# Routed attention and a gated feed-forward layer: picks over three steps, their mask factor on Pool, sums by halves, a deeper lead of scores in the first batch

## Chip, cores, metric

The kernel runs on one core of a Trainium2 chip. The metric is the time of one execution on the device in microseconds; below, the median of the runs shown is compared. The core's engines are TensorE (PE; its weight loads are listed as PEld), VectorE (DVE), ScalarE (ACT), GpSimd (POOL) and SyncE (SP, which here only issues DMAs). Each engine works through its own list of instructions in the order in which the program wrote them, and waits on semaphores for what other engines and DMAs deliver.

## What is computed

Two layers, one after the other, for 4 batches, 8 heads, 768 positions and 64 values per head:

```python
q_assign = argmax(normalised q . normalised centroids)      # 16 clusters per head
k_assign = argmax(normalised k . normalised centroids)
mask = q_assign[:, :, :, None] == k_assign[:, :, None, :]
scores = where(mask, scale * q @ k.T, -1e9)
attn = softmax(scores)                                      # + 1e-9 in the denominator
x = (attn @ v) laid out as (4 * 768, 512)
out = (sigmoid(x @ w_gate) * (x @ w_val)) @ w_out           # d_ff = 1536
```

The inputs are float32, and so is the output of 3072 x 512. The norm of q or k doesn't change which cluster wins, so only the centroids are normalised.

## The kernel before

**Steps.** The whole attention is a list of 384 steps written out by hand. A step is one block of scores: 128 keys of one head against 384 queries (`do_scores`, L467), an exp of it on ACT into an `es` tile (L472), and, some steps later, three small matmuls that add `es` times v to the head's accumulator (`do_av`, L484). A head has 12 steps, a pair of heads 24, a batch 96. `run_steps` writes for each step, in this order: the step's scores; a share of the feed-forward work that is waiting (`ffn_run`); the av of the step that lies `ahead` steps back; and then whatever was put on that step with `at(step, f)`. `ahead` is 3 in batch 0 and 2 later. The first two heads of batch 0 are interleaved (`first_steps`).

**The mask inside the scores.** Rows 64 to 79 of the transposed tile `T` of a head hold, for keys, a one-hot of the winning cluster, and for queries -1920 where the cluster is not the winning one. So the score matmul over 80 rows (128 in batch 0) adds -1920 wherever the clusters differ, and exp makes it zero. After a head's last av, `normalise` adds a tiny multiple of the sums of v (`SV`), takes the reciprocal of the sum column and scales: L235 and L236 on DVE, L237 on POOL (on DVE for the last head of batch 0). The tile `xp` of two heads is then transposed into `xT`, by DMA (L499) or, for the last pair of batch 0, by PE (`by_pe`, L507, L508).

**Preparing a pair, batches 1 to 3** (`pair_prep`, for the pair whose scores begin at step `use`, from step `s0` on, with `gap` steps between its two heads): the loads of k, q and v by SP (L111); `sp`, a split of k (side 0) or q (side 1) into a half-precision high part (L743, on DVE for the first three pairs and on POOL after that) and the remainder (L744, POOL); `turn`, a DMA transpose into `T` (L257); `lgt`, the matmuls with the centroids into one PSUM bank (L273) and a copy of their low part by ACT (L279); `pk`, the pick, all on DVE in one step: the sum of the two parts (L304), the maximum (L285), two compares into a one-hot tile (L291), and the factor -1920 on the query side (L298); `ot`, the transpose of the one-hot tile (L761 by DMA, L323 and L759 by PE for the first pair); and `hops`, four small DMAs that put the one-hots into rows 64 to 79 of the two `T` tiles (L327). `v_cast` (POOL, L187 and L188) makes the v operand, `v_sum` the sums of v: one reduction on DVE (L194) and later a matmul (L200) and a scaling (L205). `first` holds the starting steps of the first three pairs (load, `s0`, `gap`); for the others they are use-76, use-58 and 10.

**Preparing a pair, batch 0.** PE does the transposes (`turn_pe`, L595, with the copy out at L596), the picks (`a_pick`) take two heads at once and have no mask factor (it comes with the copy out, in `place` or as `slot_f` in `a_place`, L639), `a_place` transposes the one-hots on PE (L323) and hops them, and the sums of v come from PE (`v_sum_pe`, L212). The first two heads are prepared ahead of step 0 by the code at L671 to L702, with dummy matmuls (`dummies`, L558) between the parts; `split` there makes high and low parts (L572, L574), and `first_place` copies the first one-hots (L629 on DVE, L627 on ACT).

**Feed-forward.** The work of a batch is cut into atoms (`ffn_atoms`): gate matmuls (L341) and a tanh (L347, ACT), value matmuls (L356) and the product `hT` (L361, DVE), and output matmuls (L373) with copies out (L380, L382). `ffn_run` deals them out over the steps of the next batch; what is left runs after the last step. In batch 0 there are none to deal out.

**Buffers.** PSUM has a `ring` of four banks for scores, gate, value, logits and, from step 96 on, everything that `prep_bank` gives out; two banks for av; two (`op`) for outputs and, before step 96, the preparing work. `es` tiles come from a pool of 6.

The pool's depth, the lead and the order in a step are set by these lines:

```python
esp = pool("es", 6)
...
while len(pend) > ahead:
    do_av(pend.pop(0))
run_bg(step_no[0])
...
first = {96: (45, 54, 6), 120: (50, 68, 8), 144: (62, 84, 10)}
ld, s0, gap = first.get(use, (use - 76, use - 58, 10))
...
run_steps([(24, first_steps)] + heads(0)[2:], x0, 0, None, ahead=3)
```

Of the kernel before, what the change touches and what calls it, by code (L numbers as in the profile page):

```python
# [8 lines left out]
FP = mybir.dt.float32  # L9
# [7 lines left out]
def kernel(  # L17
# [11 lines left out]
    nc = tc.nc  # L29
# [27 lines left out]
    ohp = pool("oh", 2)  # L57
    esp = pool("es", 6)
    tmpp = pool("tmp", 2)
# [130 lines left out]
    def v_sum(b, p):  # L190
        s = svp.tile([128, 2, 65], HP, tag="vs", name="vs")
        POOL.memset(s[:, :, 64:65], float(NCH))
        with nc.allow_low_precision("sums of the fp16 values' sources"):
            DVE.tensor_reduce(  # L194
                s[:, :, 0:64], RAW["v", b, p].rearrange("p h c d -> p h d c"), AX.X, ALU.add
            )

        def rest():
            t = bank(130, name="vs_ps")
            PE.matmul(  # L200
                out=t, lhsT=ones, rhs=s.rearrange("p h d -> p (h d)"), start=True, stop=True
            )
# [4 lines left out]
        return rest  # L207

# [78 lines left out]

    def mark(lg, mx, parts, mask=True):

        for a, z, nh, key, o in parts:  # L290
            DVE.tensor_tensor(  # L291
                o,
                lg[:, a:z].rearrange("p (h c) n -> p h c n", h=nh),
                bcast(mx[:, a:z].rearrange("p (h c) -> p h c", h=nh), NCL),
                ALU.is_equal if key else ALU.is_lt,
            )
            if mask and not key:
                DVE.tensor_scalar(o, o, MASK, None, ALU.mult)  # L298

    def pick(lg, parts, mask=True):  # L300
        if isinstance(lg, tuple):
            ls = smp.tile([128, 12, NCL], FP, name="lgs")
            n = lg[0].shape[1]
            DVE.tensor_tensor(ls[:, 0:n], lg[0], lg[1], ALU.add)  # L304
            lg = ls[:, 0:n]
        mark(lg, top(lg), parts, mask)

# [167 lines left out]
    def do_av(s):  # L475
# [34 lines left out]
        if last_x:  # L510
            at(step_no[0] + 4, by_pe)
        elif b == 0:
            at(47 + 4 * p, by_dma)
        else:
            by_dma()
# [3 lines left out]
    def at(i, f):  # L519
        bg.setdefault(max(i, step_no[0]), []).append(f)  # L520
# [97 lines left out]
    def a_pick(p):  # L618
        oh = st0["oh", p] = new_oh()
        pick(st0["lg", p], [(0, 12, 2, True, oh_view(oh, 0, 2, 2, 6)),  # L620
                            (12, 24, 2, False, oh_view(oh, 1, 2, 2, 6))], mask=False)

# [25 lines left out]
    def first_pick(e):  # L648
        lg, oh = st0["lg0", e], ohs[0]
        mark(lg, top(lg), [(0, 6, 1, True, oh_view(oh, 2 * e, 1, 1, 6)),  # L650
                           (6, 9, 1, False, oh_view(oh, 2 * e + 1, 1, 1, 3))], mask=False)

# [10 lines left out]
    def rest_pick():  # L663
        pick(st0["lgr"], [(0, 6, 2, False, oh_view(ohs[1], 0, 2, 1, 3))], mask=False)

# [18 lines left out]
    centroid_d(cv)  # L684
    split(1, 0, 6, POOL, POOL)
    split(1, 6, 9, POOL, POOL)
    dummies(2)
    turn_pe([(0, 0, 6)], ACT)
    turn_pe([(0, 6, 3)], DVE)
    dummies(2)  # L690
    first_logits(0)
    v_cast(0, 0, ACT)
    for e in range(2):
# [25 lines left out]
    for p in range(1, NP):  # L719
# [9 lines left out]
        at(l_at[3], lambda p=p: a_pick(p))  # L729
        at(l_at[3] + 2, lambda p=p: a_place(p, (0,) if p == 1 else ()))  # L730
        at(U - 9, lambda p=p: v_cast(0, p))
        at(U - 5, lambda p=p: v_sum_pe(0, p))
# [3 lines left out]
    def pair_prep(b, p, use, s0, gap):  # L736
# [11 lines left out]

        def pk(e):
            if e == 0:  # L750
                st["oh"] = new_oh()
            pick(st["lg", e], [(0, 6, 1, True, oh_view(st["oh"], 2 * e, 1, 1, 6)),
                               (6, 12, 1, False, oh_view(st["oh"], 2 * e + 1, 1, 1, 6))])

# [11 lines left out]

        lead = 10 if gap < 10 else 12
        for e in range(2):
            s = s0 + gap * e
            at(s, lambda e=e: sp(e, 0))  # L770
            at(s + gap // 2 - 1, lambda e=e: sp(e, 1))
            at(s + gap - 1, lambda e=e: turn((b, 2 * p + e), st["hl", e], tp))
            at(s + gap + lead, lambda e=e: lgt(e))
            at(s + gap + lead + 1, lambda e=e: pk(e))
        s = s0 + 2 * gap + lead + 2
        at(s, ot)
# [3 lines left out]
        at(use - 20, lambda: v_cast(b, p))  # L780
        at(use - 15, lambda: st.update(f=v_sum(b, p)))
        at(use - 6, lambda: st["f"]())

    for b in range(1, B):
        for p in range(NP):
            use = 96 * b + 24 * p
            first = {96: (45, 54, 6), 120: (50, 68, 8), 144: (62, 84, 10)}
            ld, s0, gap = first.get(use, (use - 76, use - 58, 10))
# [50 lines left out]
```

## Time and profile before

| | |
|---|---|
| median of 8 runs | 354.46 us (354.14 to 356.18) |
| the profiled execution | 354.14 us, its span 352.4 us |
| mean granted TensorE clock | 0.985 of full speed |
| TensorE busy | 328.2 us (93% of the span) |
| ScalarE busy | 232.7 us (66%) |
| VectorE busy | 172.8 us (49%) |
| GpSimd busy | 123.3 us (35%) |
| exp of one step (L472) | 497 ns, 384 of them |
| scores of one step (L467) | 333 ns listed, 384 of them |
| split remainder (L744, POOL) | 914 ns, 48 of them |
| sums of v (L194, DVE) | 1484 ns, 12 of them |
| mask factor (L298, DVE) | 423 ns in the mean, 24 of them |
| compares of the picks (L291, DVE, 96 elements) | 325 ns in the mean, 48 of them |

How to read it: the page of the profile lists for each engine the busy time, its share of the span and the number of instructions; a table by stage does the same for stretches of the span, with the TensorE clock that was granted (1.00 is full speed) and the share of time in which the DMA engines were busy. A row of waits says which engine and line waited for which, then us in total, how often, and the longest. A row of the timeline has the start in us, the length in us, engine, line, operation, output<-input, shapes, the count, and in brackets the idle time of the engine before it and what ended that. A "q" after an engine's name is its instruction queue, so "SPq" rows are DMA issues. Matmuls overlap in the array, so the listed duration of one is longer than its share of the engine's time.

### The profile page before, as it was taken

Reading aid. Unit: us, or ns where it says so; the run is one execution under the profiler, and the core shown is the slowest. Engines: PE = TensorE matmul, PEld = TensorE weight load, DVE = VectorE, ACT = ScalarE, POOL = GpSimd, SP = SyncE. Lnnn points to the kernel's source line nnn. Section 1 sums busy time; section 2 is a strip of 40 time slices with the busy share of each in tenths; the row PEclk is TensorE's granted clock in tenths of the full one; section 3 lists DMA queues with packets and bytes.
Section 4 is the critical chain, followed back from the end, with each engine's and each line's share of the span. In section 5 each row is a group of like instructions: output and inputs, shape, how many; then the busy total and the mean of one; then the engine's idle time right before and its main releaser. Section 6 shows DMA issues by size and latency. Waiting matters only on the chain.

```text
span 352.4 us, 8568 instructions
## 1 busy us (share of the span) xinstructions
PE 328.2 (93%) x3276; PEld 203.1 (58%) x3276; DVE 172.8 (49%) x395; ACT 232.7 (66%) x533; POOL 123.3 (35%) x199
## 2 busy tenths in 40 slices
PE   7797875889999999999999999999999999999995
PEld 3476643656655665565656566556655665565552
DVE  5486643765564547346554566455634232342230
ACT  5676875787867787677867787578876884332321
POOL 4896464335353445314353535333211000000000
PEclk9999997799999999999999999999999999999999
DMA  7999999495473398666765299433413010300102
GB/s 215 331 201 211 270 216 237 96 218 175 102 220 80 95 220 223 106 124 182 102 180 128 92 225 198 116 87 69 78 25 96 30 24 10 103 1 32 60 0 89
DMA packets 81000, 46.44 MB, mean 132 GB/s; under 512 B 60832, under 2 KB 77888, under 8 KB 80960
## 3 DMA queue, kind: packets, MB, share of 16 engines
q1 hardware_dynamic: 76960, 40.99, 47.7%
q0 software_dynamic: 3712, 4.72, 7.9%
q8 instruction: 25, 0.41, 0.5%
q10 hardware_dynamic: 288, 0.20, 0.2%
q14 instruction: 15, 0.12, 0.1%
HBM read 28.34 MB, written 6.29 MB: 98 GB/s over the span
## 4 chain that ended last, share of the span: by engine, by line
PE 73%; DVE 5%; DMA 3%; issue 2%; ACT 1%; POOL 1%; DVEq 0%; POOLq 0%
PE o L373 17%; PE v L356 17%; PE g L341 17%; PE sc L467 12%; PE av L484 7%; DMA T<-hl 3%; DVE hT L361 2%; PE lg L273 2%; DVE oh L291 1%; DMA T<-ohT 1%; DVE mx L285 1%; DVE t L235 0%; DVE lgs L304 0%; ACT th L347 0%; DVE vs L194 0%
## 5 line engine op out<-in xcount | busy, mean ns | idle before, releaser
L472 ACT ACTIVATE es<-sc 128x384 f16<-128x384 f32 x384 | 173.8, 497 | 53.0 <-PE sc L467 37.1
L467 PE MATMUL sc<-T 80*128 80x384 f16 (+1 forms) x384 | 119.8, 333 | 3.2 <-DVE hT L361 1.8
L484 PEld LDWEIGHTS <-es 128*128 128x128 f16 x1152 | 82.5, 99 | 47.4 <-ACT es L472 3.6
L361 DVE SCALAR_TENSOR_TENSOR hT<-th,v 128x384 f16<-128x384 f32 x96 | 52.8, 553 | 98.9 <-PE av L484 57.9
L484 PE MATMUL av<-va,es 128*128 128x65 f16 x1152 | 99.2, 196 | 0.0
L356 PE MATMUL v<-xTb,wv 128*128 128x384 f16 x384 | 78.1, 325 | 1.7 <-DVE hT L361 1.3
L237 POOL TENSOR_TENSOR xp<-t,rec 128x384 f16<-128x384 f32 x31 | 25.7, 830 | 150.2 <-DVE rec L236 145.1
L341 PE MATMUL g<-xTb,wg 128*128 128x384 f16 x384 | 78.0, 325 | 0.3
L373 PE MATMUL o<-wo,hT 128*128 128x512 f16 x288 | 70.6, 378 | 0.0
L347 ACT ACTIVATE th<-g 128x384 f32<-128x384 f32 x96 | 47.4, 494 | 26.6 <-DVE hT L361 16.2
L341 PEld LDWEIGHTS <-wg 128*128 128x128 f16 x384 | 37.3, 97 | 24.5 <-issue 3.2
L356 PEld LDWEIGHTS <-wv 128*128 128x128 f16 x384 | 37.3, 97 | 23.7 <-issue 3.5
L373 PEld LDWEIGHTS <-hT 128*128 128x128 f16 x288 | 27.9, 97 | 25.5
L467 PEld LDWEIGHTS <-T 80*128 80x128 f16 (+1 forms) x384 | 37.5, 98 | 0.6 <-DVE T L629 0.5
L744 POOL TENSOR_TENSOR hl<-qraw,hl 128x384 f16<-128x384 f32 x24 | 21.9, 914 | 13.1 <-DVE hl L743 11.6
L382 ACT ACTIVATE ob<-o 128x512 f32<-128x512 f32 x16 | 9.6, 598 | 22.3 <-PE o L373 22.3
L744 POOL TENSOR_TENSOR hl<-kraw,hl 128x384 f16<-128x384 f32 x24 | 21.9, 913 | 4.6 <-PE av L484 1.7
L235 DVE TENSOR_TENSOR t<-av,sv 128x390 f32<-128x390 f32 x32 | 18.0, 562 | 11.2 <-PE av L484 9.8
L194 DVE TENSOR_REDUCE vs<-vraw 128x128 f16<-128x768 f32 x12 | 17.8, 1484 | 0.0
L380 DVE TENSOR_SCALAR ob<-o 128x512 f32<-128x512 f32 x8 | 5.5, 692 | 22.2 <-PE o L373 22.2
L273 PE MATMUL lg<-cm,T 128*128 128x32 f16 x288 | 11.0, 177 | 4.1 <-DMA T<-hl 4.1
L304 DVE TENSOR_TENSOR lgs<-lg,lglo 128x192 f32<-128x192 f32 x24 | 8.2, 343 | 12.6 <-ACT lglo L279 12.3
(84 smaller groups left out, 216.0 us busy)
## 6 DMA issues: line engine op xcount, KB each, us to landing
vraw<-in_v_dram SPq DMA_DIRECT2D x16, 384.0 KB, 5.4
out_dram<-ob SPq DMA_DIRECT2D x24, 256.0 KB, 2.2
kraw<-in_k_dram SPq DMA_DIRECT2D x15, 384.0 KB, 3.8
qraw<-in_q_dram SPq DMA_DIRECT2D x15, 384.0 KB, 4.3
wg<-in_moe_w_gate_dram POOLq DMA_DIRECT2D x2, 768.0 KB, 10.3
wv<-in_moe_w_val_dram POOLq DMA_DIRECT2D x2, 768.0 KB, 13.3
wo<-in_moe_w_out_dram POOLq DMA_DIRECT2D x4, 384.0 KB, 15.6
T<-ohT SPq DMA_DIRECT2D x58, 24.0 KB, 1.9
```

Source lines behind the costliest of these rows:

```text
L235: DVE.tensor_tensor(t, av, sv, ALU.add)
L237: eng.tensor_tensor(x, t[..., 0:64], bcast(r, 64), ALU.mult)
L273: PE.matmul(out=lg[:, bass.ts(c, 32)], lhsT=t[:, c, :], rhs=cm[:, h].rearrange("p s n -> p (s n)"), start=True, stop=True,)
L341: PE.matmul(out=g[:, 0:n], lhsT=wg[fc // WQ][:, dc, fc % WQ, :], rhs=xT[:, dc, t0 : t0 + n], start=(dc == 0), stop=(dc == NDC - 1),)
L347: ACT.activation(th[:, 0:n], g[:, 0:n], AF.Tanh, scale=0.5)
L356: PE.matmul(out=w[:, 0:n], lhsT=wv[fc // WQ][:, dc, fc % WQ, :], rhs=xT[:, dc, t0 : t0 + n], start=(dc == 0), stop=(dc == NDC - 1),)
L361: DVE.scalar_tensor_tensor(hT[:, fc, 0:n], st[0][:, 0:n], 1.0, w[:, 0:n], ALU.add, ALU.mult)
L373: PE.matmul(out=o, lhsT=hT[:, fc, bass.ts(t, 128)], rhs=wo[fc // 3][:, fc % 3, :], start=(fc == 0), stop=(fc == NFC - 1),)
L467: PE.matmul(out=sc.rearrange("p (c t) -> p c t", t=128), lhsT=s["k"], rhs=s["q"], start=True, stop=True,)
L472: ACT.activation(es, sc, AF.Exp, scale=SCALE)
L484: PE.matmul(out=av[:, s["c0"] + i, :], lhsT=s["es"][:, bass.ts(i, 128)], rhs=VA[b, p][:, e, s["j"], :], start=(first and i == 0), stop=(la ...
L744: POOL.tensor_tensor(hl[:, :, 64:128], r, hl[:, :, 0:64], ALU.subtract)
```

## The change

1. **Picks of batches 1 to 3 in three steps.** `pk` no longer runs in one step: in the first, the sum and the maximum (L304, L285); in the second, the compare of the key side; in the third, the compare of the query side, and its factor -1920, which moves from VectorE to GpSimd. `mark` and `pick` lose their mask argument. `ot` follows two steps later, and so do the hops. `lead`, the steps from a head's transpose to its logits, becomes 12 for all pairs (it was 10 where `gap` is under 10), and the `gap` of the first pair of batch 1 becomes 5.
2. **Sums of v by halves.** `v_sum` reduces one head at use-17 and the other at use-14, in place of both at use-15. GpSimd's small memset moves to use-17 with it.
3. **First batch.** `ahead` is 4 (3 before), the pool of `es` tiles has 7. `a_place` comes 5 steps after the pick (3 for the second pair; it was 2), `v_cast` 18 steps before the pair's end of preparation (it was 9), and the PE transposes of the last `xp` five steps after it (it was 4).
4. **Before step 0.** The high parts of the second head's first k and q parts are made by ACT (POOL before), two single dummies stand where two pairs stood, the copy of the first transposed k goes to DVE (ACT before), and the second head's q part is split after the first logits.

```diff
-    esp = pool("es", 6)
+    esp = pool("es", 7)
...
-        with nc.allow_low_precision("sums of the fp16 values' sources"):
-            DVE.tensor_reduce(
-                s[:, :, 0:64], RAW["v", b, p].rearrange("p h c d -> p h d c"), AX.X, ALU.add
-            )
+
+        def half(e):
+            with nc.allow_low_precision("sums of the fp16 values' sources"):
+                DVE.tensor_reduce(
+                    s[:, e, 0:64], RAW["v", b, p][:, e].rearrange("p c d -> p d c"), AX.X, ALU.add
+                )
...
-            if mask and not key:
-                DVE.tensor_scalar(o, o, MASK, None, ALU.mult)
...
-            at(step_no[0] + 4, by_pe)
+            at(step_no[0] + 5, by_pe)
...
-    split(1, 0, 6, POOL, POOL)
-    split(1, 6, 9, POOL, POOL)
-    dummies(2)
-    turn_pe([(0, 0, 6)], ACT)
+    split(1, 0, 6, ACT, POOL)
+    dummies(1)
+    turn_pe([(0, 0, 6)], DVE)
     turn_pe([(0, 6, 3)], DVE)
-    dummies(2)
+    dummies(1)
     first_logits(0)
+    split(1, 6, 9, ACT, POOL)
     v_cast(0, 0, ACT)
...
-        at(l_at[3] + 2, lambda p=p: a_place(p, (0,) if p == 1 else ()))
-        at(U - 9, lambda p=p: v_cast(0, p))
+        at(l_at[3] + (3 if p == 1 else 5), lambda p=p: a_place(p, (0,) if p == 1 else ()))
+        at(U - 18, lambda p=p: v_cast(0, p))
...
-        def pk(e):
-            if e == 0:
+        def pk(e, i):
+            if e == 0 and i == 0:
                 st["oh"] = new_oh()
-            pick(st["lg", e], [(0, 6, 1, True, oh_view(st["oh"], 2 * e, 1, 1, 6)),
-                               (6, 12, 1, False, oh_view(st["oh"], 2 * e + 1, 1, 1, 6))])
+            if i == 0:
+                st["ls", e] = total(st["lg", e])
+                st["mx", e] = top(st["ls", e])
+            elif i == 1:
+                mark(st["ls", e], st["mx", e],
+                     [(0, 6, 1, True, oh_view(st["oh"], 2 * e, 1, 1, 6))])
+            else:
+                o = oh_view(st["oh"], 2 * e + 1, 1, 1, 6)
+                mark(st["ls", e], st["mx", e], [(6, 12, 1, False, o)])
+                POOL.tensor_scalar(o, o, MASK, None, ALU.mult)
...
-        lead = 10 if gap < 10 else 12
+        lead = 12
...
-            at(s + gap + lead + 1, lambda e=e: pk(e))
-        s = s0 + 2 * gap + lead + 2
+            for i in range(3):
+                at(s + gap + lead + 1 + i, lambda e=e, i=i: pk(e, i))
+        s = s0 + 2 * gap + lead + 4
...
-        at(use - 15, lambda: st.update(f=v_sum(b, p)))
-        at(use - 6, lambda: st["f"]())
+        at(use - 17, lambda: st.update(f=v_sum(b, p)))
+        at(use - 17, lambda: st["f"][0](0))
+        at(use - 14, lambda: st["f"][0](1))
+        at(use - 6, lambda: st["f"][1]())
...
-            first = {96: (45, 54, 6), 120: (50, 68, 8), 144: (62, 84, 10)}
+            first = {96: (45, 54, 5), 120: (50, 68, 8), 144: (62, 84, 10)}
...
-    run_steps([(24, first_steps)] + heads(0)[2:], x0, 0, None, ahead=3)
+    run_steps([(24, first_steps)] + heads(0)[2:], x0, 0, None, ahead=4)
```

More of the change, by code (lines that the diff above doesn't have):

```diff
@@ L205, in rest @@
             DVE.tensor_scalar(sv.rearrange("p h d -> p (h d)"), t, TINY, None, ALU.mult)
-        return rest
+        return half, rest
     def v_sum_pe(b, p):
@@ L286, in top, with mark @@
         return mx
-    def mark(lg, mx, parts, mask=True):
+    def mark(lg, mx, parts):
         for a, z, nh, key, o in parts:
@@ L296, in mark, with total, pick @@
             )
-            if mask and not key:
[L298 to L306, printed above, removed]
+    def total(lg):
+        ls = smp.tile([128, 12, NCL], FP, name="lgs")
+        n = lg[0].shape[1]
+        DVE.tensor_tensor(ls[:, 0:n], lg[0], lg[1], ALU.add)
+        return ls[:, 0:n]
+    def pick(lg, parts):
+        mark(lg, top(lg), parts)
     oh_n = [0]
@@ L620, in a_pick @@
         pick(st0["lg", p], [(0, 12, 2, True, oh_view(oh, 0, 2, 2, 6)),
-                            (12, 24, 2, False, oh_view(oh, 1, 2, 2, 6))], mask=False)
+                            (12, 24, 2, False, oh_view(oh, 1, 2, 2, 6))])
     def place(t, ps, slot, c0, n, key, eng):
@@ L650, in first_pick @@
         mark(lg, top(lg), [(0, 6, 1, True, oh_view(oh, 2 * e, 1, 1, 6)),
-                           (6, 9, 1, False, oh_view(oh, 2 * e + 1, 1, 1, 3))], mask=False)
+                           (6, 9, 1, False, oh_view(oh, 2 * e + 1, 1, 1, 3))])
     def first_place(e):
@@ L663, in rest_pick @@
     def rest_pick():
-        pick(st0["lgr"], [(0, 6, 2, False, oh_view(ohs[1], 0, 2, 1, 3))], mask=False)
+        pick(st0["lgr"], [(0, 6, 2, False, oh_view(ohs[1], 0, 2, 1, 3))])
     def rest_place():
```

## The prediction

> **What bounds the kernel now.** I read the page's engine shares first, then a table by stage, then who waits for whom on TensorE, and last two stretches of the timeline. The page says that TensorE is the engine to watch:
>
> ```profile
> PE 328.2 (93%) x3276; PEld 203.1 (58%) x3276; DVE 172.8 (49%) x395; ACT 232.7 (66%) x533; POOL 123.3 (35%) x199
> PEclk9999997799999999999999999999999999999999
> ```
>
> By stage (stretch, then busy us and count of PE, PEld, DVE, ACT, POOL, granted clock, DMA share, GB/s), with cuts at the first score, before and after the worst hole, at the full feed-forward load and at the last attention step:
>
> ```profile
> 12.00:52.00 40.00, 33.55 (x576) 25.09 (x575) 25.89 (x59) 30.01 (x69) 28.48 (x40) 1.00 1.09 235
> 52.00:72.00 20.00, 14.40 (x181) 10.13 (x180) 10.82 (x31) 13.16 (x32) 9.12 (x13) 0.74 0.72 169
> 90.00:296.00 206.00, 202.04 (x1993) 125.02 (x1992) 102.89 (x225) 152.80 (x356) 71.89 (x118) 1.00 0.53 120
> ```
>
> Busy overstates TensorE, so I also went through the starts of its matmuls. Back to back they lie 0.162 us apart for 384 columns, 0.216 for 512, 0.030 for the 65-column av; time beyond that I call lost. Lost: 5.1 us in 0-12, 10.5 in 12-52, 10.4 in 52-72 (half clock included), 1.9 in 72-90, 8.4 in 90-296, 0.1 after: 36.4 of 352.4. This is all that a change of order can give back. In batch 0 (steps 0-95, to 72 us) there is no feed-forward work to fill holes; a plain step there runs at ScalarE's pace, (3.95-0.49)/9 = 0.384 us per exp (ten in 3.95 us), against 0.25 us of TensorE.
>
> Later batches: one pick in two puts a clump on VectorE.
>
> ```profile
> 100.05 0.84 DVE L291 TENSOR_TENSOR oh<-lgs,mx 128x96 f16<-128x96 f32 x2
> 100.86 0.91 POOL L744 TENSOR_TENSOR hl<-kraw,hl 128x384 f16<-128x384 f32 x1
> 100.92 0.89 DVE L298 TENSOR_SCALAR oh<-oh 128x96 f16<-128x96 f16 x1
> 101.73 1.01 DVE L361 SCALAR_TENSOR_TENSOR hT<-th,v 128x384 f16<-128x384 f32 x2
> 102.33 0.32 PE L467 MATMUL sc<-T 80*128 80x384 f16 x1 [0.61 <-DVE hT L361]
> ```
>
> The mask L298 needs 0.19 us alone and 0.89 beside Pool's L744; two hT are held behind it, their PSUM banks stay taken, and TensorE waits. I count such holes at 101, 138, 159, 178, 197, 215, 236 and 256 us: 6.3 of the 8.4 us lost there.
>
> Batch 0 ends with the other large hole. SyncE's queue and what waits for it:
>
> ```profile
> 48.09 2.43 SPq L327 DMA_DIRECT2D T<-ohT  x4
> 50.61 1.91 SPq L257 DMA_TRANSPOSE T<-hl  x1
> 52.57 0.57 SPq L111 DMA_DIRECT2D kraw<-in_k_dram  x1
> 53.20 0.50 SPq L111 DMA_DIRECT2D qraw<-in_q_dram  x1
> 53.75 0.46 SPq L111 DMA_DIRECT2D vraw<-in_v_dram  x1
> 54.33 2.64 SPq L257 DMA_TRANSPOSE T<-hl  x1
> ```
>
> ```profile
> PE lg L273 <- DMA T<-hl: 4.1, 3, 3.4
> PE vs_ps L212 <- POOL va L188: 2.5, 2, 1.6
> PE oh_ps L323 <- DVE oh L291: 2.4, 3, 0.8
> ```
>
> SyncE issues without a pause; the last transpose lands 6.25 us after its issue (the chain of waits), at 60.6, and the logits of step 76 stand on TensorE from 57.1 to 60.6. The other two rows (us, times, longest) are a_place and v_sum_pe, which come before their data.
>
> **What the Trainium skill says.** "SBUF — State Buffer", section Who interferes with whom: VectorE and GpSimd share one port pair under an exclusive lock; a two-port-mode op or one with two SBUF inputs blocks fully against a Pool instruction, a tensor_reduce never. The trace agrees: L298 is 188 ns at its fastest and 893 at its slowest, L291 245 and 552, L194 always 1471 to 1496. "Perfetto Trace Analysis", per-instruction lifecycle, DMA HWDGE: an issue's profiled window is not the transfer; here 2.64 us against 6.25. "TensorE: Matmul & The Clock Gate", What's actually happening: after an idle window the array runs at half rate; here the granted clock is 0.74 in 52-72.
>
> **The change, part by part.**
>
> Picks. There are 24. L298 leaves VectorE: 10.2 us in total. On Pool it is an operation the trace lacks (96 halves from SBUF, one input). Lower bound 0.17 us (the 128x12 memset L187), upper 0.55 (the 192-element two-input L574); from Pool's casts L572 (344 ns at 192, 527 at 384) I take 344-96x0.95 = 0.25, so 6 us on an engine 35% busy. It waits there for mark's second compare. Queued behind it are the next pair's L743/L744, three steps later; their transpose is due 5 steps after those, their logits 18, so nobody waits. At the first head of each pair VectorE now runs t 0.56, rec 0.19, lgs 0.32, mx 0.35, two oh 0.84, mask 0.89 = 3.2 us ahead of the next hT. After: 1.4 us in the first step, then a compare of 0.26 (up to about 1.1 if locked out by L744) in each of the next two, an hT able to go between. The one pick with no Pool work beside it (256 us, 2.0 us of clump) lost 0.31, and the second heads' picks of about 1.3 us lost nothing, so about 1.7 us are free. I keep 0.15 us per place, 8 x 0.15 = 1.2 of 6.3, and round the gain to **5.0**. The bounds are all of it, 6.3, and minus 3.5 (rival 3). The one-hot transpose and hops move two steps later; hops still issue 11 steps (9 us) before use and land in 2-4 us: 0.
>
> Sums. L194 becomes two. The fixed part from L285: 353 ns at 192 elements, 554 at 384 (another row of that line) gives 152; a half is (1484-152)/2+152 = 0.82 us. VectorE pays 12x0.15 = 1.8 us in all, hidden (49% busy). It was on the path once, at 78-81 us, where TensorE lost 0.29: gain **0.3**.
>
> Prologue. Two dummies go (0.43 us of PE); the k copy moves from ACT (0.78) to DVE (0.55); ACT takes casts of 0.51 and 0.35, Pool sheds 0.64 and 0.34. The first score (11.57) waits for ACT's place L627 at 11.04, which is queued behind casts that waited for q's DMA until 10.09. ACT's queue is as long as before (0.86 for 0.78) and still reaches those casts early. Gain **0**; from -0.3 to +0.4.
>
> Batch 0 to step 54. a_place(1) one step later, a_place(2) and (3) three; v_cast nine steps earlier. Holes at 25.1 (0.98), 27.3 (1.49), 33.7 (0.95) and 38.4 (1.06) would shrink to some 0.9 in all; those at 45.9 and 50.6 come after. But head 4's hops now leave later by step. The pick is done at 34.66, or about 33.0 once 1.7 us are saved before it; step 36's transposes, ohT (0.62) and two issues put the second hop at 35.2; hops there take 4.6 us to land (DMA share over 1): 39.8, when step 48's score was at 41.54. So the first 3.6 us are capped: **1.5** (0.5 to 3.5). A fourth score ahead covers 4x0.384 = 1.54 us of TensorE's absence for ScalarE instead of 1.15, which helps only up to the same landing.
>
> Step 54 to 76. Pool takes v_cast (0.97 us) before the splits, in a gap it had (2.57 us idle before 43.8). SyncE now issues the first transpose, then four hops, then three loads, then the second transpose: 1.9+2.4+1.6 us as before, starting when q's low part is ready, 3.4 us after step 54, where the hops started before (48.1). So the second transpose again issues near 9.6 and lands near 15.8 us after step 54's start. TensorE arrives at step 76 earlier (holes of 0.95, 1.79 and 0.51 gone, 3.2 us) and waits that much longer: **0**. Step 72 now waits for hops queued behind the transpose, inside the same wait.
>
> Step 76 to 104. The one-hot transposes lost 1.12 and will wait some 0.3; but the logits of the next pair's second head, two steps later, again meet their transpose (issued after the hops, landing about 10.6 us after step 76): **0.4**. The last xp of batch 0 no longer stands behind a pick on VectorE, and its transposes come one step later: 0.81 lost becomes 0.3: **0.5**.
>
> Sum: 5.0+0.3+0+1.5+0+0.4+0.5 = 7.7 us. The profiled execution took 354.14 us (span 352.4 and 1.7 around it), 0.3 below the median of 354.46; 354.14-7.7 = **346.4**.
>
> **Rivals.**
> 1. Batch 0 is not tied to SyncE. For: 20.9 us are lost in 12-72; against: six queue entries without a gap. If hops and transposes keep up, the 3.6 and 3.2 us both count, less the 1.5 already in: 346.4-5.3 = **341.1**.
> 2. The steady gain is only half: compares locked out by L744 at 0.9 us still delay hT. For: Pool's split begins one step after the first-head pick. 346.4+2.5, and nothing from batch 0 (+1.5): **350.4**; without any steady gain, 353.5, near no change.
> 3. Slower: the port lock at the second heads. Their compares move to the steps in which Pool starts the next pair's split, where formerly they were over. t, rec, then a compare of 0.26+0.9 is 1.9 us, with a mask on Pool after it. If the clump at both heads goes past about 2.5 us, each first head keeps its 0.8 and each second head gains one of 0.4: 8x0.4 = 3.2 more lost, batch 0 nothing: **357**. It decides when the compares, not the mask, are what Pool blocks.
>
> **Numbers.** Main case 0.57, rival 1 0.20, rival 2 0.13 (0.02 of it within 0.2%), rival 3 0.10. A measurement of this kernel can tell about 0.2%, 0.7 us. Faster 0.88, same 0.02, slower 0.10. Low end: rival 1's price, 341.1; high end: rival 2 with almost no gain left, 352.5. Left out: rival 3 and what is beyond rival 1.
>
> **What would show it.** Right: L298's line on Pool near 0.25 us, no TensorE wait for hT over 0.3 us in 90-290, lost time there near 3 us; SyncE again unbroken before the second T<-hl, a wait on it of 5 us or more at step 76, half clock once more after it. Wrong: logits of step 76 not waiting for the transpose (rival 1), L291 near 1 us and hT waits as before (rivals 2 and 3), or a first score not at 11.6.

## Result and the profile after

The changed kernel takes **349.51 us** in the median (11 runs, 348.97 to 351.79), the kernel before 354.54 us (32 runs). The ratio is 0.986 [0.9841, 0.988]: about 5.0 us faster, inside the range of the prediction, but 2.7 us less than its 7.7. In one of the experiments below (the loads behind the turn) the profiled execution was disturbed, so its time and its profile are not used.

The profiled execution has a span of 347.3 us (352.4 before), which is again 5.1 us. The page's engine shares and its line of granted clocks, after:

```profile
PE 325.4 (94%) x3274; PEld 203.7 (59%) x3274; DVE 160.2 (46%) x384; ACT 232.5 (67%) x534; POOL 134.7 (39%) x221
PEclk9999896799999999999999999999999999999999
```

VectorE has lost 12.6 us of work and Pool has taken 11.4. Neither number is the gain. The table by stage shows where time went (stretch, then busy us and count of PE, PEld, DVE, ACT, POOL, granted clock, DMA share, GB/s):

```profile
12.00:50.20 38.20, 32.84 (x562) 25.76 (x559) 23.57 (x58) 28.16 (x65) 26.20 (x37) 0.96 1.14 239
50.20:67.00 16.80, 9.98 (x123) 7.09 (x121) 7.68 (x21) 9.69 (x24) 8.41 (x13) 0.70 0.77 164
85.00:291.00 206.00, 205.49 (x2050) 128.01 (x2049) 95.50 (x224) 156.55 (x366) 84.59 (x141) 1.00 0.53 126
```

The last row answers to 90 to 296 us of before: of 206 us TensorE is now busy in 205.49, where it was 202.04, and runs 57 more matmuls in the same time. The first two rows are no better than before: the clock is 0.96 where it was 1.00, and 0.70 where it was 0.74.

The starts of single scores put numbers on this. Score n is the block of scores of step n, counted from 0; lengths are between starts, in us:

| from score to score | before | after | gained | forecast |
|---|---|---|---|---|
| start to 54 | 44.34 | 45.89 | -1.55 | +1.5 |
| 54 to 77 (the long wait of step 76 in it) | 16.62 | 16.31 | +0.31 | 0 |
| 77 to 105 | 15.64 | 14.47 | +1.17 | +0.9 |
| 105 to 383 | 217.09 | 211.93 | +5.16 | +5.3 |
| 383 to the last matmul | 54.73 | 54.73 | 0 | 0 |
| sum | 348.42 | 343.33 | +5.09 | +7.7 |

So the whole shortfall lies in the first row. TensorE's lost time, counted as in the prediction, falls from 36.4 to 31.8 us. Between scores 105 and 383 the same matmuls run before and after (2120 in each by the table by stage), so the 5.16 us by which that stretch got shorter are lost time that has gone: 9.01 us become 3.85.

**The first-head pick, after.** The timeline where a clump of 3.2 us stood on VectorE, its rows of VectorE and Pool alone:

```profile
98.39 0.56 DVE L237 TENSOR_TENSOR t<-av,sv 128x390 f32<-128x390 f32 x1 [1.00 <-PE av L486]
98.99 0.19 DVE L238 RECIPROCAL rec<-t 128x6 f32<-128x6 f32 x1
99.10 0.32 DVE L304 TENSOR_TENSOR lgs<-lg,lglo 128x192 f32<-128x192 f32 x1
...
99.45 0.35 DVE L287 TENSOR_REDUCE mx<-lgs 128x12 f32<-128x192 f32 x1
...
99.72 0.54 DVE L363 SCALAR_TENSOR_TENSOR hT<-th,v 128x384 f16<-128x384 f32 x1
...
100.18 0.63 DVE L293 TENSOR_TENSOR oh<-lgs,mx 128x96 f16<-128x96 f32 x2
...
100.61 0.97 POOL L746 TENSOR_TENSOR hl<-kraw,hl 128x384 f16<-128x384 f32 x1
...
101.30 0.56 DVE L363 SCALAR_TENSOR_TENSOR hT<-th,v 128x384 f16<-128x384 f32 x1 [0.48 <-PE av L486]
...
101.67 0.45 POOL L763 TENSOR_SCALAR oh<-oh 128x96 f16<-128x96 f16 x1
```

An hT (L363) now goes between the maximum and the compares, 1.3 us after the chain began, and the next one waits for its own data, not for VectorE. L293 lists two compares in one row. The factor (L763) sits on Pool behind the split.

**Batch 0, after.** Who waits for whom on TensorE (us in total, times, longest), some of the first rows:

```profile
PE lg L275 <- DMA T<-hl: 7.0, 3, 4.9
PE sc L469 <- DMA T<-ohT: 2.2, 1, 2.2
PE sc L469 <- ACT T L629: 1.6, 1, 1.6
...
PE sc L469 <- DVE T L633: 1.1, 1, 1.1
PE sc L469 <- ACT es L474: 0.9, 2, 0.6
```

The waits of before for `va` (2.5 us), those of the one-hot transposes for VectorE (2.4) and those for hT have gone from this list, which takes idle times of over 0.15 us. Three shorter ones for hT are left, at 138.15, 213.09 and 251.89 us. In their place the logits wait longer for the transposes (7.0 us for 4.1), and the second and fourth rows are new: score 48 waits for hops, and score 24 for the copies by which VectorE places a head's one-hots (L633). At that place TensorE's transposes waited for VectorE before:

```profile
PE t_ps L595 <- DVE ohT L639: 1.3, 1, 1.3
```

SyncE's queue after the change, from the hops of head 4 on:

```profile
36.09 2.40 SPq L329 DMA_DIRECT2D T<-ohT  x4
...
49.74 1.40 SPq L259 DMA_TRANSPOSE T<-hl  x1
51.23 2.85 SPq L329 DMA_DIRECT2D T<-ohT  x4
54.14 0.57 SPq L111 DMA_DIRECT2D kraw<-in_k_dram  x1
54.76 0.46 SPq L111 DMA_DIRECT2D qraw<-in_q_dram  x1
55.27 0.47 SPq L111 DMA_DIRECT2D vraw<-in_v_dram  x1
55.84 5.30 SPq L259 DMA_TRANSPOSE T<-hl  x2
```

From 49.74 to 61.1 the queue works without a pause, in the order that the prediction gave: transpose, four hops, three loads, transpose. The chain of waits holds both ends:

```profile
36.69 4.75 DMA T<-ohT
41.43 0.14 issue
41.57 0.48 PE sc L469
...
49.74 4.37 DMA T<-hl
...
55.84 5.97 DMA T<-hl
61.86 0.52 PE lg L275 x12
```

The hops land 4.75 us after the second issue and let step 48's score go at 41.57; the second transpose lands 5.97 us after its issue and lets step 76's logits go at 61.86.

### The profile page after: what moved, and what is told of

Read it like the earlier page. It is cut to its first block, busy times and chain, and to the rows that moved or that the text cites. A ratio compares the mean times of both kernels' runs of the same rounds, so it can differ in the third digit from the quotient of the medians.

```text
span 347.3 us, 8525 instructions
## 1 busy us (share of the span) xinstructions
PE 325.4 (94%) x3274; PEld 203.7 (59%) x3274; DVE 160.2 (46%) x384; ACT 232.5 (67%) x534; POOL 134.7 (39%) x221
## 4 chain that ended last, share of the span: by engine, by line
PE 85%; DMA 7%; DVE 4%; ACT 1%; issue 1%; SPq 1%; POOL 1%; POOLq 0%; DVEq 0%
PE g L343 18%; PE v L358 18%; PE o L375 18%; PE sc L469 16%; PE av L486 9%; DMA T<-hl 4%; PE lg L275 2%; DMA qraw<-in_q_dram 2%; PE t_ps L597 1%; DMA T<-ohT 1%; PE lg L612 1%; PE oh_ps L325 1%; DVE hT L363 0%; DVE mx L287 0%; PE wm L560 0%
## 5 line engine op out<-in xcount | busy, mean ns | idle before, releaser
L474 ACT ACTIVATE es<-sc 128x384 f16<-128x384 f32 x384 | 173.7, 499 | 44.9 <-PE sc L469 33.2
L363 DVE SCALAR_TENSOR_TENSOR hT<-th,v 128x384 f16<-128x384 f32 x96 | 53.2, 554 | 101.2 <-PE av L486 60.2
L237 DVE TENSOR_TENSOR t<-av,sv 128x390 f32<-128x390 f32 x32 | 18.0, 562 | 13.7 <-PE av L486 13.4
L196 DVE TENSOR_REDUCE vs<-vraw 128x64 f16<-128x384 f32 x24 | 19.2, 815 | 0.0
L281 ACT COPY lglo<-lg 128x192 f32<-128x192 f32 x24 | 7.8, 325 | 12.1 <-PE lg L275 12.1
## 6 DMA issues: line engine op xcount, KB each, us to landing
wg<-in_moe_w_gate_dram POOLq DMA_DIRECT2D x2, 768.0 KB, 11.4
wo<-in_moe_w_out_dram POOLq DMA_DIRECT2D x4, 384.0 KB, 15.8
```

The source lines that it names most:

```text
L196: DVE.tensor_reduce(s[:, e, 0:64], RAW["v", b, p][:, e].rearrange("p c d -> p d c"), AX.X, ALU.add)
L237: DVE.tensor_tensor(t, av, sv, ALU.add)
L363: DVE.scalar_tensor_tensor(hT[:, fc, 0:n], st[0][:, 0:n], 1.0, w[:, 0:n], ALU.add, ALU.mult)
L474: ACT.activation(es, sc, AF.Exp, scale=SCALE)
```

## The experiments

Twelve kernels. Ratios are to the kernel before, run beside them. Line numbers in the kernels that keep the old batch 0 are close to those of before; in the others they are those of after.

| kernel | median us | ratio |
|---|---|---|
| picks alone | 348.65 | 0.983 [0.9802, 0.9858] |
| all but the picks | 355.97 | 1.0035 [1.0019, 1.0051] |
| picks spread, factor left on VectorE | 348.85 | 0.9841 [0.9814, 0.9869] |
| factor on Pool, pick in one step | 350.38 | 0.9883 [0.9858, 0.9908] |
| after, loads behind the turn | 345.87 | 0.9754 [0.9726, 0.9783] |
| after, direct place | 350.37 | 0.9875 [0.9847, 0.9902] |
| after, both of these | 345.55 | 0.9755 [0.9725, 0.9784] |
| picks alone, loads behind the turn | 348.1 | 0.9814 [0.9786, 0.9843] |
| after, old start | 349.28 | 0.9858 [0.9829, 0.9886] |
| after, lead of three | 350.94 | 0.9868 [0.9843, 0.9894] |
| both, and more dummies | 345.5 | 0.974 [0.9709, 0.9771] |
| the same, and late weights | 351.62 | 0.9925 [0.9893, 0.9957] |

**1. The picks alone.** The kernel before with part 1 of the change, without its edits of `lead` and of the first `gap`.

```diff
-            at(s + gap + lead + 1, lambda e=e: pk(e))
-        s = s0 + 2 * gap + lead + 2
+            for i in range(3):
+                at(s + gap + lead + 1 + i, lambda e=e, i=i: pk(e, i))
+        s = s0 + 2 * gap + lead + 4
...
+                POOL.tensor_scalar(o, o, MASK, None, ALU.mult)
```

> The kernel before with the pick in three steps, its factor on Pool, and the one-hot transpose and hops two steps later; nothing else of the change. Theory 1 (the whole gain is made in batches 1 to 3, because no hT is held behind a pick any more): 5.2 us faster than before, 349.3, ratio 0.985, and no wait of TensorE for hT of 0.3 us or more; score 105 at 76.6 us as before. Theory 2 (the edits of the first batch carry part of the gain): 2 to 3 us faster, 351.5 to 352.5.

Measured 348.65 us, 0.983 [0.9802, 0.9858]. Between scores 105 and 383 TensorE loses 3.83 us (9.01 before), and its list of waits has none for hT. The picks carry the whole gain.

**2. All but the picks.** The changed kernel with the pick in one step again and its factor on VectorE.

```diff
...
+            pick(total(st["lg", e]), [(0, 6, 1, True, oh_view(st["oh"], 2 * e, 1, 1, 6)),
+                                      (6, 12, 1, False, o)])
+            DVE.tensor_scalar(o, o, MASK, None, ALU.mult)
...
```

> The changed kernel with the old pick: one step, the factor on VectorE, the one-hot transpose two steps after it. Theory 1: no gain, 354.5, within 0.8 of before; score 48 waits for the hops and score 77 for the second transpose as in the changed kernel, and the holes behind hT (6 us between 85 and 300) are back. Theory 2: 2 to 3 us faster than before.

Measured 355.97 us over 22 runs, 1.0035 [1.0019, 1.0051]: alone, the other three parts cost some 1.2 us. Steps 105 to 383 take 216.81 us, 0.28 less than before. The waits of TensorE name the rest:

```profile
PE lg L275 <- DMA T<-hl: 9.1, 2, 5.0
PE sc L469 <- ACT T L629: 2.2, 1, 2.2
PE sc L469 <- DVE hT L363: 1.8, 3, 0.6
PE sc L469 <- DMA T<-ohT: 1.5, 1, 1.5
```

The waits for hT are those of before (1.8, 3 times, longest 0.6). The logits wait 9.1 us for the transposes, for 4.1 before.

**3. Picks spread, factor on VectorE.** The same as kernel 1, but for one line.

```diff
-                POOL.tensor_scalar(o, o, MASK, None, ALU.mult)
+                DVE.tensor_scalar(o, o, MASK, None, ALU.mult)
```

> As the first run of this call, but the factor stays on VectorE, in the third step. If the length of the clump on VectorE is what counts (an hT can go between), nearly all of the gain stays: 349.5 to 350.5, although the factor still takes 0.9 us beside a Pool instruction. If the lock between VectorE and Pool is what counts, 1 to 2 us of gain at most: 352.5 to 353.5.

Measured 348.85 us, 0.9841 [0.9814, 0.9869], the same as kernel 1 within the intervals. The row of its groups (count, then busy us and mean ns of one, idle before):

```profile
L761 DVE TENSOR_SCALAR oh<-oh 128x96 f16<-128x96 f16 x24 | 17.4, 726 | 0.8
```

The factor is even more held up beside Pool than it was (726 ns in the mean, 423 before), which agrees with the port sharing that the prediction took from the Trainium skill ("SBUF — State Buffer", Who interferes with whom: that page says "fully blocks" of the two-port modes, and of an op with two SBUF inputs only that it contends with a Pool instruction that reads SBUF), and yet steps 105 to 383 lose only 4.04 us. What counted was that hT stood behind a long clump, not the blocked instruction as such; moving the factor to Pool is not needed once the pick is spread.

**4. Factor on Pool, pick in one step.** The kernel before, with the factor after the pick, on Pool.

```diff
-                               (6, 12, 1, False, oh_view(st["oh"], 2 * e + 1, 1, 1, 6))])
+                               (6, 12, 1, False, o)], mask=False)
+            POOL.tensor_scalar(o, o, MASK, None, ALU.mult)
```

> The kernel before with only the factor moved to Pool; the pick stays in one step. If the length of the clump counts: it falls from 3.2 to 2.3 us, still above the 1.7 that seem free, so about half of the gain: 351.5 to 352.5. If the lock counts: all of it, 349.5.

Measured 350.38 us, 0.9883 [0.9858, 0.9908], faster than the 351.5 to 352.5 expected. The timeline of VectorE at its first-head pick:

```profile
100.51 0.57 DVE L235 TENSOR_TENSOR t<-av,sv 128x390 f32<-128x390 f32 x1 [1.00 <-PE av L484]
...
101.96 0.53 DVE L291 TENSOR_TENSOR oh<-lgs,mx 128x96 f16<-128x96 f32 x2
102.41 0.54 DVE L361 SCALAR_TENSOR_TENSOR hT<-th,v 128x384 f16<-128x384 f32 x1
```

The clump is 102.41-100.51 = 1.9 us long, since the two compares take 0.53 us here, not the 0.84 of before; hT comes after it. Of the two holes that TensorE had at such a place before, the one of 0.77 us behind hT has gone; one of 0.23 us stays, in front of a value matmul that waits for ACT's tanh (L347), as it did before (100.81 us there, 102.72 here). Steps 105 to 383 lose 4.51 us in all, 0.7 more than with the spread, and three more of these holes for ACT make up that 0.7. So the factor's move alone brings most of the steady gain, and either edit is enough against the waits for hT. The rest of the 1.7 us between this kernel and kernel 1 lies elsewhere in part: from score 76 to score 80 TensorE loses 5.84 us here and 3.18 there.

**5. Loads behind the turn.** The changed kernel, with three loads of 384 KB each put two steps later, behind the second transpose in SyncE's queue.

```diff
-            first = {96: (45, 54, 5), 120: (50, 68, 8), 144: (62, 84, 10)}
+            first = {96: (45, 54, 5), 120: (50, 68, 8), 144: (64, 84, 10)}
```

> The changed kernel, but the three loads of the third pair of batch 1 are written at step 64 and not at 62, so behind the second DMA transpose on SyncE's queue. Theory (step 77 is tied to SyncE's queue: the transpose is issued 1.6 us late and lands behind 1.15 MB of loads): that transpose is issued near 54.2 us and lands some 4 us later, score 77 starts near 58.5 in place of 62.2, and the kernel is 2.5 to 3.5 us faster than the changed one, 346 to 347. Rival (the transpose waits for the splits on Pool and VectorE, the loads beside it cost nothing): 349.5, score 77 stays near 62.

Measured 345.87 us in five runs (345.12 to 346.99), 0.9754 [0.9726, 0.9783]: some 3.7 us better than the change, for one number in a table. This is the tie of batch 0 to SyncE, shown by taking it away; kernels 7 and 8 below show the same edit in their traces.

**6. Direct place.** The changed kernel with the one-hots of every pair's first head put into `T` by VectorE, in place of hops, so that step 48 needs none for that head.

```diff
-        at(l_at[3] + (3 if p == 1 else 5), lambda p=p: a_place(p, (0,) if p == 1 else ()))
+        at(l_at[3] + (3 if p == 1 else 5), lambda p=p: a_place(p, (0,)))
```

> The changed kernel, but the one-hots of the first head of the third and fourth pair of batch 0 are placed by two VectorE copies, as those of the second pair are, and not by hops. Theory (step 48 is tied to the landing of the hops, and the hole there halves the clock afterwards): score 48 doesn't wait, no half clock near 41 to 45 us, score 54 near 43 in place of 45.9, and the kernel is 2 to 3 us faster than the changed one, 346.5 to 347.5. Rival (ScalarE sets the pace there and takes back what TensorE gains): within 0.7 of 349.5.

Measured 350.37 us, 0.9875 [0.9847, 0.9902]: no gain where 346.5 to 347.5 was expected. A miss. Its waits of TensorE say why:

```profile
PE lg L275 <- DMA T<-hl: 7.2, 2, 3.6
PE sc L469 <- DMA T<-ohT: 2.5, 1, 2.5
```

Step 48 no longer waits. Step 36 does, for head 3's hops, which the edit doesn't touch: the second was issued at 31.36 and landed 6.5 us later, and TensorE lost 2.62 us there. In the changed kernel (issue at 29.92, landing 4.6 us later) it lost 0.73. Half clock at 38.7 us followed. So nothing was won up to step 54, which starts at 46.82, and scores 54 to 77 still take 17.1 us.

**7. Both.** The edits of kernels 5 and 6 together.

> Both edits of the two runs before in one kernel. If both ties are real and independent: 5 to 6 us faster than the changed kernel, 343.5 to 344.5, score 105 near 71. If the one hides the other: as the better of the two alone, 346.5.

Measured 345.55 us, 0.9755 [0.9725, 0.9784]: no more than kernel 5 alone, where 343.5 to 344.5 was expected. In its profile step 48 starts at 39.66 and step 54 at 42.45, which is 1.9 us earlier than before; scores 54 to 77 take 13.9 us.

SyncE's queue in this kernel:

```profile
46.58 2.76 SPq L259 DMA_TRANSPOSE T<-hl  x1
49.45 1.84 SPq L329 DMA_DIRECT2D T<-ohT  x2
51.39 1.42 SPq L259 DMA_TRANSPOSE T<-hl  x1
52.86 0.58 SPq L111 DMA_DIRECT2D kraw<-in_k_dram  x1
```

The second transpose goes 4.8 us after the first (6.1 in the changed kernel), with the loads behind it. But the first one now lands so late that the logits of step 71 wait 4.2 us for it: it is issued into loads that keep the DMA engines busy up to 50 us (share 1.17 from 41.6 to 50.2 us in the changed kernel too).

**8. Picks alone, loads behind the turn.** Kernel 1 with the edit of kernel 5, to the same place in its own order.

```diff
-            first = {96: (45, 54, 6), 120: (50, 68, 8), 144: (62, 84, 10)}
+            first = {96: (45, 54, 6), 120: (50, 68, 8), 144: (66, 84, 10)}
```

> The kernel before with the three-step pick alone, and the loads of the third pair of batch 1 at step 66 and not at 62, behind the second transpose (step 65 there). Theory (SyncE's queue): 2.5 to 3.5 us faster than the three-step pick alone, 345 to 346, so ahead of the changed kernel by 4. Rival: 348.7, as the three-step pick alone.

Measured 348.1 us, 0.9814 [0.9786, 0.9843]: 0.55 us better than kernel 1, not 2.5 to 3.5. Another miss. The tie does break, since scores 54 to 77 take 13.7 us for 16.4 in kernel 1; but 77 to 105 take 17.3 us for 14.8, and a wait of TensorE has grown, from 0.7 us in kernel 1:

```profile
PE oh_ps L323 <- POOL oh L761: 2.1, 1, 2.1
```

The one-hot transposes of the next pair now stand for the factor, which starts at 61.24. Pool's queue holds `va` and a split (60.11 to 61.03) ahead of it, and the compare before it ends last, at 61.15: beside that split it took 0.96 us, where the fastest takes 0.22. This is the lock-out of a compare that the prediction allowed for ("up to about 1.1"), in batch 0 and not in the steady state. Kernel 7 has the same wait:

```profile
PE oh_ps L325 <- POOL oh L763: 1.5, 1, 1.5
```

So it explains the missing gain only in part. Half clock at 61.4 and 71.6 us is in this profile too (3.4 us each), and how much each took stays open. Set against kernel 5, this run also prices parts 2 to 4 of the change, with its edits of `lead` and of the first `gap`, once the tie is broken: 0.9754 [0.9726, 0.9783] with them, 0.9814 [0.9786, 0.9843] without, intervals that just miss each other, about 2.2 us. So they are worth something that the changed kernel itself can't show. Which of them it is, no run separates.

**9. The old start.** The changed kernel with part 4 undone.

```diff
-    split(1, 0, 6, ACT, POOL)
-    dummies(1)
-    turn_pe([(0, 0, 6)], DVE)
+    split(1, 0, 6, POOL, POOL)
+    split(1, 6, 9, POOL, POOL)
+    dummies(2)
+    turn_pe([(0, 0, 6)], ACT)
     turn_pe([(0, 6, 3)], DVE)
-    dummies(1)
+    dummies(2)
     first_logits(0)
-    split(1, 6, 9, ACT, POOL)
```

> The changed kernel with the part ahead of step 0 as in the kernel before (two pairs of dummies, casts on Pool, the copy of k on ScalarE). Two of five profiles with the new part have a half clock of 3.4 us near 12 us, none of five with the old one. If the dropped dummies cost something: 0.5 to 1 us faster than the changed kernel, 348.5 to 349, and no half clock near 12. If not: 349.5.

Measured 349.28 us, 0.9858 [0.9829, 0.9886], against 0.986 [0.9841, 0.988] with it: part 4 is worth nothing that these runs can tell, and the intervals leave room for about 1 us either way.

**10. A lead of three.** The changed kernel with the old `ahead` in batch 0.

```diff
-    run_steps([(24, first_steps)] + heads(0)[2:], x0, 0, None, ahead=4)
+    run_steps([(24, first_steps)] + heads(0)[2:], x0, 0, None, ahead=3)
```

> The changed kernel with a lead of three scores in batch 0 in place of four. Theory (batch 0 is tied to the hops and to SyncE's queue): no effect, 349.5 within 0.7. Rival (the fourth score hides about 0.4 us of each of the six holes of TensorE): 1.5 to 2.5 us slower, 351 to 352.

Measured 350.94 us, 0.9868 [0.9843, 0.9894]: 1.4 us more in the median, but the ratio differs by 0.0008 from the changed kernel's. Not decided: the fourth score is worth between nothing and that 1.4 us.

**11. Both, with more dummies.** Kernel 7 with two dummies where the change has one, twice, and eight for three ahead of the first score, to see whether a busier start keeps the clock up later.

```diff
-    dummies(1)
+    dummies(2)
...
-    dummies(1)
+    dummies(2)
...
-    dummies(3)
+    dummies(8)
```

> The kernel with direct placing and the loads behind the transpose, and the two pairs of dummies back, eight dummies in place of three ahead of the first score. If the idle stretch before the first score costs clock in some executions: 344.5 to 345, half a microsecond to one faster than without them (345.55). If not: 345.5.

Measured 345.5 us, 0.974 [0.9709, 0.9771]: as kernel 7 within the intervals. The dummies do nothing that these runs can tell. With kernel 7 it is the best version measured.

**12. The same, with late weights.** The four loads of the output weights (384 KB each) from steps 9 to 24 to steps 97 to 109, out of the time in which hops land slowly.

```diff
-        at(9 + 5 * i, lambda i=i: load_wo(i))
+        at(97 + 4 * i, lambda i=i: load_wo(i))
```

> As the run before, with the four loads of the output weights at steps 97 to 109 and not 9 to 24. If what is left in batch 0 is the traffic of the DMA engines (their share is 0.9 or more from 0 to 45 us), the hops and the first transpose land earlier and the kernel is 1 to 2 us faster than the run before, 343 to 344; a logits wait of 4 us at step 71 shrinks to under 2. If it is not traffic but the order of the queue: no change.

Measured 351.62 us, 0.9925 [0.9893, 0.9957]: 6 us slower than kernel 11, where 1 to 2 us faster was expected. SyncE's queue at the place where it goes wrong:

```profile
66.57 0.47 SPq L111 DMA_DIRECT2D vraw<-in_v_dram  x1
67.14 4.55 SPq L259 DMA_TRANSPOSE T<-hl  x1
72.19 3.27 SPq L771 DMA_TRANSPOSE ohT<-oh  x1
75.55 2.52 SPq L259 DMA_TRANSPOSE T<-hl  x1
```

In kernel 11 the same first transpose takes 2.31 us to issue, the one after it 1.72. Here it is 4.55, with weights issued at 66.6, 73.1 and 73.9 us, and it lands 11.2 us after its issue: TensorE loses 5.04 us in one hole at 73.4 us, in front of the logits that read it. Early on the move helps: head 3's hops land 3.3 to 3.8 us after their issue (4.7 to 6.2 in kernel 11), no score waits for hops, and step 48 starts at 40.5 (42.4 in kernel 11). So the traffic went from hops that cost 2 us to a transpose that costs 5.

## Why the prediction was right and where it was wrong

**The picks: right, in place and size.** The step "one pick in two puts a clump on VectorE, hT is held behind it" gave 5.0 us, and steps 105 to 383 gained 5.16. Kernel 1, which has the picks alone, gains 5.18 there, and kernel 2, which lacks them, 0.28. The holes of 0.77 to 0.85 us are gone from the trace; what stays above 0.25 us is 0.31 us at three places. The claim that lost time would be near 3 us was a little low (3.85).

**The length of the clump: right in direction, its price misread.** "About 1.7 us are free" was read from the hole of 0.31 us behind a clump of 2.0 us at 256 us. That hole is there after the change as well, at 251.89, with the clump spread out: its hT waits for TensorE, in both kernels. So that clump cost nothing, and in kernel 4 clumps of 1.9 us leave no hole of 0.77 to 0.85 us either. What the prediction kept, "0.15 us per place", 1.2 us in all, is near what stays (three holes of 0.31 and one of 0.23 us), but these holes aren't the picks': the 5.0 came so close partly by luck. And the blocked mask is not the cause as such: left on VectorE at 726 ns (kernel 3), with hT free to go between, it costs nothing.

**The factor on Pool.** Estimated at 0.25 us, bounds 0.17 to 0.55. The group's row of the changed kernel:

```profile
L763 POOL TENSOR_SCALAR oh<-oh 128x96 f16<-128x96 f16 x24 | 10.9, 453 | 11.7 <-DVE oh L293 10.1
```

0.45 us, within the bounds but nearly twice the value taken, since it was scaled from a cast of more elements by its slope. In the steady state nobody waits for it, as said. In batch 0 somebody does: 0.3 us in the changed kernel, 1.5 in kernel 7, 2.1 in kernel 8.

**The sums by halves.** 815 ns each, estimated 820. The 0.3 us of gain is not shown to be theirs. Kernel 2, which has them without the picks, is 0.28 us shorter between scores 105 and 383, and the hole of 0.29 us at 81 us is gone in it; but it is gone in kernels 1, 3 and 4 too, which leave the sums whole.

**The start.** Forecast 0, and kernel 9 finds nothing else, within about 1 us. The first score comes at 11.29 for 11.57, and still waits for ACT's place (L629).

**Batch 0 to step 54: wrong, and all of the shortfall.** The prediction saw the right cap, the landing of head 4's hops, and set it at 39.8 us, "the second hop at 35.2" plus 4.6. The landing was right (4.75), the issue was not: 36.69. Two things made it late.

The step that failed is "the pick is done at 34.66, or about 33.0 once 1.7 us are saved before it". It was over at 34.31, only 0.35 us before its old time, and scores 25 to 31 start 0.35 us earlier too, no more. The holes of 0.98 and 1.49 us at 25.1 and 27.3 were to shrink; they became three, of 0.69, 1.25 and 0.47 us. The longest stands in front of score 24. VectorE, which places the first head's one-hots for that score, makes its two copies at 27.34 and 27.92 (26.96 and 27.52 before), and score 24 waits for the second until 28.53. The prediction moved `a_place` and put down nothing for these copies. In the profiles of kernels 2, 6, 7, 9, 11 and 12 this wait is 1.1 us too. No run takes it away, so how much it alone costs stays open.

The second is small. `a_place` now stands at step 36 (33 before), behind that step's score, and this score waited until 34.65 for the hops of the head before, head 3, which landed at 34.52. The list of waits puts it down to an exp (L474, at 34.53), but the exp that had to free the score's PSUM bank, that of step 32, was over at 33.77. In kernels 2, 6, 7, 9, 10 and 11 score 36 starts 0.13 to 0.14 us after the same landing too, anywhere from 34.44 to 38.01 us, and kernel 9's list names the hops at both steps, 36 and 48:

```profile
PE sc L469 <- DMA T<-ohT: 2.7, 2, 1.6
```

So `a_place`'s transposes started at 34.90 (34.72 before), its hops at 36.09 (35.92 before). What TensorE had won (0.9 us at step 36, and more after it) was given back in one wait of 2.2 us, and step 48 started where it had started before, 41.57 for 41.54. The term of 1.5 was 0.

Then the wait had a price of its own. These are the stage rows of the changed kernel from 36 us on:

```profile
36.00:41.60 5.60, 3.40 (x55) 2.72 (x54) 3.18 (x8) 3.93 (x11) 3.22 (x4) 0.98 1.23 224
41.60:50.20 8.60, 8.57 (x138) 6.80 (x139) 5.04 (x13) 6.66 (x16) 3.98 (x6) 0.81 1.17 296
```

TensorE is busy 3.40 us of 5.60, and after it runs at 0.81 for 8.6 us: half clock from 41.4 to 44.8. Steps 48 to 54 take 4.32 us, 2.80 before: 1.5 us lost. That is 0 - 1.5 = -1.5 in place of +1.5. The Trainium skill, "TensorE: Matmul & The Clock Gate", What's actually happening, says that the gate watches a free-running window of about 3.4 us; the trace agrees, with half-clock stretches of 3.41, 6.83, 10.24 and 13.65 us in the runs here, in different places in kernels that are equal up to there. So this second 1.5 us is partly a draw: kernel 1 and kernel 8 are the same program up to step 61, and one starts step 54 at 45.86 with half clock at 28.6 us, the other at 44.55 without. But the gain itself is missing in all four profiles with the changed kernel's `a_place`: this one and kernels 2, 9 and 10 start step 54 between 45.62 and 46.00, and TensorE waits 1.5 to 2.7 us for hops in each. Three of them have a half-clock stretch at 11 to 12 us in place of the one at 41. That no gain came is shown; that every execution loses 1.5 us on top is not. The mean granted clock of every run is on record: 0.985 over 27 runs of the kernel before, 0.9815 over the changed kernel's 12, 0.9775 over kernel 2's 22. Half clock for 3.41 us takes 0.005 off the mean of a span of 350 us, so by estimate the changed kernel has some 0.8 of a stretch more than before. Kernel 5, the changed kernel but for the loads, is back at 0.988 over five runs, so the stretch may as well come with the long wait of step 76.

**Steps 54 to 76: right as a tie; the size is less firm.** The step "the second transpose again issues near 9.6 and lands near 15.8 us after step 54's start" measured 9.95 and 15.9 (61.8 less 45.89). The logits waited 4.87 us. From score 54 to 77 it is 16.6 us before, 16.3 after, 16.4, 17.0, 17.2 and 17.1 in kernels 1, 3, 4 and 6. It is more in kernels 2, 9 and 10, 19.2, 18.2 and 18.3, where the transpose is issued 11.6 to 12.5 us after step 54's start and lands 17.8 to 18.8 after it, though kernel 9 is the changed kernel from step 0 on. So the predicted 9.6 and 15.8 fit one execution better than all. But with the loads behind the transpose the stretch is 12.8 to 13.9 us (kernels 7, 8, 11 and 12), and the two groups don't overlap. A distance that never falls under 16.3 us whatever else the kernels change, and that gives way to one reordering, is what a tie looks like. Rival 1 (not tied, 341.1) is out.

**Steps 77 to 105: right in sum**, 1.17 us for 0.9.

**Rivals 2 and 3** are out by steps 105 to 383: no wait for hT over 0.31 us is left, and no compare takes over 0.55 us. Yet the time of rival 2, 350.4, lies nearer to the 349.51 measured than the forecast of 346.4 does. It would have been met for the wrong reason: its half-lost steady gain didn't happen, its "nothing from batch 0" did. (Its price without any steady gain, 353.5, should be 353.2 by its own terms, 346.4 with 5.0, 0.3 and 1.5 added.)

## What to carry to other kernels

Before you count a saving, walk the whole chain behind it to the instruction that ends the stage, with the queue in front of each link: here the gain before step 54 needed the hops to leave earlier, and they stood behind VectorE's copies for score 24 and the landing of the hops before them; and the gain up to step 76 needed a transpose, which was tied to three loads that nobody needed yet. Where a distance between two points doesn't shrink while the kernel around it changes, move what stands in front of its last link: one number in a table of starting steps brought 3.7 us, three quarters as much as the whole change. And an operation that is dear on an engine does no harm by its length, but by what it holds up; letting the urgent instruction go between was enough.

## What the hardware showed that was not expected

- A DMA transpose is slow when loads run: 4.4 us from issue to landing at 49.7 us, 6.0 us behind three loads, 3.25 and 3.40 us for the same one with the loads behind it (kernels 7 and 8), and an issue of 4.55 us where the output weights were loading, 2.31 us where they were not.
- A scaling of 128 x 96 half-precision elements on Pool takes 453 ns (448 at the fastest, 493 at the slowest), hardly less than its casts of 384 elements (0.50 us at 100 us), so the cost of a small operation there can't be had by scaling elements.
- Half clock came at 11 to 12 us in four profiles (kernels 2, 6, 9 and 10), with the new start's two dummies as with the old start's four, and in neither of the two with eight ahead of the first score (11 and 12). The medians of kernels 7 and 11 show no gain from more dummies.
